# Four attention layers on one core: the first chunk's queries and keys by way of HBM, a reordered beginning, and dense rows for three output projections

## Chip, core and metric

The kernel runs on one core of a Trainium2 chip, alone. The metric is the device time of one execution in microseconds (us); several executions are timed and their median is given. A core has TensorE (matmuls; "PE" in a profile, its weight loads "PEld"), VectorE ("DVE"), ScalarE ("ACT"), GpSimd ("POOL") and SyncE ("SP", which here only issues transfers). Each engine works through its own list of instructions in order, and waits for others by semaphores. SBUF is the on-chip memory, PSUM the memory that matmuls write (eight banks here), HBM the memory outside.

## What is computed

Four layers, each with its own layernorm and a residual: windowed attention (A), full attention (B), A again, B again, over 2048 positions and 640 features, with 32 heads of 20 features. A and B each have one set of weights, used twice.

```
H = 32; Dh = D // H; W = 256                                # D = 640, S = 2048
q, k, v = (x @ wqkv) split by heads
scores = einsum("bhqd,bhkd->bhqk", q, k) * (Dh ** -0.5)
...
mask = (idx[:, None] - idx[None, :] >= 0) & (idx[:, None] - idx[None, :] < W)   # A only
p = softmax(scores)
o = einsum("bhqk,bhkd->bhqd", p, v)
return o.transpose().reshape(B, S, D) @ wo
...
x = A_x
x = x + A(layernorm(x)); x = x + B(layernorm(x))
x = x + A(layernorm(x)); x = x + B(layernorm(x))
```

## The kernel before

**Tiling.** Positions are cut into four chunks of 512 (C), heads into eight groups of four (G). A *unit* (class Unit) is one layer, one chunk of queries and one group: its scores are computed key by query, so that keys lie on the partitions, ACT takes the exponential straight out of PSUM (L1462), and a second matmul with the values (L1495) gives the outputs of four heads, each on 20 of 32 partitions, with the sum of the exponentials on a 21st. The four heads of a group use the four 32-row strips of TensorE at once. For that, the queries and keys of a group lie in a tile of 128 partitions as four strips of 32 rows, 20 with data and 12 with zeros (tiles qa and ka in windowed layers, qt and kt in full ones).

**Order.** One list of units is worked through tile by tile, a tile being three or two banks of scores (an odd tile of layer 0 has two). Layers are interleaved: first the eight units of layer 0, chunk 0, then those of chunk 1; from unit (0, 1, 7) on, the first units of layer 1 alternate with those of chunks 2 and 3, and so on. For each tile the program writes out scores, exponentials, background work, and the values of an earlier tile. Each engine then runs its list in that order; what is written first is done first.

**Background work.** Norms (t_ln), values (t_v), projections to queries and keys (t_block, and t_qk_first for the first chunk) and output projections (t_out) are generators in a queue, todo, sorted by when they are due less a lead (push). pump advances them by an amount per tile: 1.2 units per tile until layer 1's first unit (function rate, before "woven"), and less afterwards. If a unit needs something that isn't written out yet, require writes out tasks until it is there. A yield of ("wait", n) puts a task aside for n tiles. The work after a unit's last values is a tail (t_tail): reciprocals of the sums, spread over the partitions, and a multiplication (L1203), two groups at a time.

**First chunk of layer 0.** first_ln writes out the first norm by hand: statistics on VectorE, the power on POOL, the scaling on ACT, transposes on TensorE, and between them matmuls that nothing reads (warm, L1262). The projections to queries and keys are made group by group by t_qk_first with weights padded to strips of 32 columns (get_w: a POOL memset and a VectorE copy from raw, which lies in the tile spare, to wqk). They land in qa and ka from PSUM by one ACT copy (evac, L345), with no transfer. There are eight groups, so sixteen projections of 5 x 4 matmuls with 512 columns.

**All other chunks.** t_block projects 128 of the 640 rows at a time with unpadded weights, five blocks each for queries and keys. The result goes from PSUM to a staging tile st, and by a transfer on POOL's queue (L566) to HBM (q_d, k_d). load_unit later issues eight transfers on SP's queue per windowed unit (L802, L803), one per head for queries and keys, which place 20 rows into each strip. load_ahead issues them as soon as a unit's blocks are written out and a buffer is free (four qa, eighteen ka).

**Output projection.** t_out works in eight half rows of a chunk (128 positions by 320 features). With padded rows, the outputs of each of the eight groups lie in a slot of the tile on, and the weights wop have zeros in the rows 20 to 31 of each strip; a half row takes 8 x 4 matmuls. With dense rows (function packed: chunks 1 to 3 of layer 3), settle moves the rows of each head by transfers on SP's queue (L1216) into the first five slots of on, and a half row takes 5 x 4. Settling waits two tiles before it issues and eight more after a chunk's last group. Until then a group's raw rows lie in slots 5 to 7, by turns.

**Loads at the start.** SP's queue issues x of chunk 0, the layer A weights in six pieces, the value weights, x of chunks 1 to 3, and the value weights of B, one after the other. t_zeros later writes zeros by POOL's queue into wop and the tiles kt and qt, and loads wop.

## Time and profile before

| | us |
|---|---|
| median of 3 runs | 2161.4 (2161.15 to 2162.79) |
| the profiled execution | 2161.74 |
| its span, first to last instruction | 2160.0 |
| first score matmuls of layer 0 | 16.29 |
| first output projection, first and last addition to x (L598) | 100.06 and 112.33 |
| first score matmul of layer 1 | 148.23 |
| second, third and fourth output projection, first addition | 196.74, 292.43, 386.60 |

The page of the profile gives busy time and share of the span of each engine. In a row by stage there are the stretch, its length, then the busy time of PE, PEld, DVE, ACT and POOL with the number of instructions in brackets, then the granted clock of TensorE (1.00 is full), the share of the transfer engines that is busy, and GB/s. In a row of the timeline there are the start, the time taken by the group of like instructions, engine, line, what is written from what, the count, and in square brackets the idle time before it and what ended that. A row on transfers ends with the KB of one and the median time from issue to landing, where the trace has it; for SP's transfers it has none.

The exponentials alone, by stage (same columns, ACT only):

```profile
16.30:33.70 17.40, 8.98 (x12) 1.00 0.22 75
33.70:86.00 52.30, 32.04 (x45) 1.00 0.48 150
86.00:98.00 12.00, 9.35 (x9) 0.86 0.16 41
98.00:113.00 15.00, 9.33 (x8) 1.00 0.06 16
113.00:155.00 42.00, 30.95 (x25) 1.00 0.19 55
155.00:196.00 41.00, 38.80 (x35) 1.00 0.32 93
```

### The profile page before, as it was taken

The page shows a single profiled execution, that of the slowest core. Times are in us where ns is not written, and L with a number is a line of the kernel's source. Part 1 is how long each engine was busy: PE and PEld are TensorE (multiplying, and loading weights), DVE is VectorE, ACT ScalarE, POOL GpSimd, SP SyncE. Part 2 cuts the span into 40 slices and gives each one's busy share as a digit, 9 for nine tenths or more (in the row PEclk, how much of TensorE's full clock was granted, in tenths as well). Part 3 has the DMA queues.
Part 4 walks back from the last instruction along what each step waited for, and adds up shares of the span by engine and source line. Part 5 has one row for each costly group of instructions (what it writes and reads, how often), then busy time and mean ns, then how long its engine had stood idle before and what let it go on. Part 6 is the DMA issues. An engine that isn't in the chain of part 4 may idle for free. (4 is left out here: it accounts for less than half of the span.)

```text
span 2160.0 us, 73146 instructions
## 1 busy us (share of the span) xinstructions
PE 1926.8 (89%) x31790; PEld 757.8 (35%) x31791; DVE 1467.3 (68%) x2613; ACT 2088.0 (97%) x1717; POOL 361.5 (17%) x805
## 2 busy tenths in 40 slices
PE   8899999988889898888988989888898988888898
PEld 4444443433333333333333433342332222222222
DVE  6556665426666776776767743773588888987886
ACT  7889899999999999999999999999999999999997
POOL 6543434000022002400033001500000000000000
PEclk9999999999999999999999999999999999999999
DMA  6212122222110222111120122111111111111100
GB/s 204 65 54 75 54 62 69 67 63 59 55 42 27 63 53 69 38 31 48 50 83 27 33 60 75 33 45 52 54 57 44 36 36 42 32 33 39 44 27 17
DMA packets 81440, 114.33 MB, mean 53 GB/s; under 512 B 20990, under 2 KB 63070, under 8 KB 81118
## 3 DMA queue, kind: packets, MB, share of 16 engines
q1 hardware_dynamic: 71502, 81.06, 14.2%
q0 software_dynamic: 9616, 28.59, 3.8%
q8 instruction: 249, 4.08, 0.8%
q14 instruction: 73, 0.60, 0.1%
HBM read 76.58 MB, written 27.79 MB: 48 GB/s over the span
## 5 line engine op out<-in xcount | busy, mean ns | idle before, releaser
L1462 ACT ACTIVATE pt<-ps 128x1536 bf16<-128x1536 f32 (+2 forms) x1641 | 2054.0, 1417 | 38.5 <-PE ps L1436 28.9
L1436 PE MATMUL ps<-qt,kt 32*128 32x512 bf16 x3913 | 543.6, 384 | 62.8 <-ACT pt L1462 55.7
L315 PE MATMUL ps<-masks,ident 128*32 128x512 bf16 x5684 | 507.6, 384 | 94.7 <-ACT pt L1462 49.1
L1495 PE MATMUL ps<-pt,vt 128*21 128x512 bf16 x3784 | 377.1, 386 | 0.3 <-ACT pt L1462 0.2
L1436 PEld LDWEIGHTS <-kt 32*128 32x128 bf16 x3913 | 155.5, 91 | 460.1 <-issue 440.8
L315 PEld LDWEIGHTS <-ident 128*32 128x32 bf16 x5684 | 182.2, 94 | 283.4 <-issue 256.7
L1535 POOL TENSOR_SCALAR_AFFINE_SELECT pt<-pt 128x256 bf16<-128x256 bf16 (+2 forms) x508 | 219.0, 453 | 198.6 <-ACT pt L1462 185.8
L348 DVE CAST st<-ps 128x512 bf16<-128x512 f32 x134 | 92.6, 691 | 144.8 <-PE ps L315 144.5
L1495 PEld LDWEIGHTS <-vt 128*21 128x21 bf16 x3784 | 93.7, 89 | 254.2 <-issue 250.5
L315 PE MATMUL ps<-wop,on 128*32 128x320 bf16 x3712 | 160.7, 300 | 4.5 <-DVE x_sb L598 2.6
L1007 DVE TENSOR_SCALAR spare<-ps 128x512 int32<-128x512 f32 x200 | 137.2, 686 | 27.8 <-PE ps L989 24.1
L315 PEld LDWEIGHTS <-on 128*32 128x32 bf16 x5760 | 122.8, 95 | 62.3 <-issue 28.4
L1546 DVE TENSOR_TENSOR pt<-pt,masks 128x256 bf16<-128x256 bf16 (+3 forms) x270 | 117.0, 449 | 39.5 <-ACT pt L1462 37.6
L1436 PE MATMUL ps<-qa,ka 32*128 32x384 bf16 (+2 forms) x1408 | 118.5, 275 | 22.9 <-ACT pt L1462 19.6
L1203 DVE TENSOR_TENSOR on<-on,ps 128x512 bf16<-128x512 bf16 x128 | 86.4, 684 | 59.0 <-PE ps L315 56.9
L598 DVE TENSOR_TENSOR x_sb<-x_sb,ps 128x320 bf16<-128x320 bf16 x120 | 58.3, 486 | 100.3 <-PE ps L315 99.5
L315 PE MATMUL ps<-wv,xnT 128*32 128x320 bf16 x2560 | 117.1, 303 | 9.5 <-DVE on L1203 3.0
L315 PE MATMUL ps<-xnT,spare 128*32 128x512 bf16 x1720 | 118.0, 381 | 5.5 <-DVE on L1203 1.8
L315 PE MATMUL ps<-xnT,wqk 128*32 128x512 bf16 x1600 | 107.7, 381 | 4.6 <-DVE rts L1182 1.3
L1007 DVE TENSOR_SCALAR raw_o<-ps 128x512 int32<-128x512 f32 x112 | 76.8, 686 | 47.6 <-PE ps L1436 46.7
L900 DVE CAST on<-ps 128x512 bf16<-128x512 f32 x112 | 76.7, 685 | 35.5 <-PE ps L1495 28.5
L566 POOL DMA_DIRECT2D k_d<-st x75 | 41.6, 555 | 270.9 <-DVE st L348 248.0
(103 smaller groups left out, 1731.6 us busy)
## 6 DMA issues: line engine op xcount, KB each, us to landing
vt<-v_d SPq DMA_DIRECT2D x48, 336.0 KB
kt<-k_d SPq DMA_DIRECT2D x192, 80.0 KB
k_d<-st POOLq DMA_DIRECT2D x75, 128.0 KB, 2.2
q_d<-st POOLq DMA_DIRECT2D x75, 128.0 KB, 2.1
qt<-q_d SPq DMA_DIRECT2D x384, 20.0 KB
v_d<-vs POOLq DMA_DIRECT2D x16, 336.0 KB, 3.0
qa<-q_d SPq DMA_DIRECT2D x224, 20.0 KB
ka<-k_d SPq DMA_DIRECT2D x224, 20.0 KB
```

Of the source, the lines that this page charges most:

```text
L315: nc.tensor.matmul(out_[r], lhsT=lhsT[:, r], rhs=rhs, start=start, stop=stop)
L348: nc.vector.tensor_copy(out=out_, in_=in_)
L566: nc.gpsimd.dma_start(out=dst, in_=staging.pop())
L598: nc.vector.tensor_tensor(out=xv, in0=had, in1=yp, op=ALU.add)
L900: nc.vector.tensor_copy(out=oT, in_=op)
L1007: nc.vector.tensor_scalar(out=xi.bitcast(I32)[:, i * C : (i + 1) * C], in0=z, scalar1=SCALE * LOG2E * FIX, scalar2=127.5 * FIX, op0=ALU.mu ...
L1203: nc.vector.tensor_tensor(out=oT, in0=oT, in1=zb, op=ALU.mult)
L1436: nc.tensor.matmul(sp[:, i, col * P : (col + qn) * P], lhsT=u.k(kc, j), rhs=u.q(j, q0, qn), start=True, stop=True,)
L1462: nc.scalar.activation(out=pt[:, i:k, b0 * P :], in_=sp[:, i:k, b0 * P :], func=ACT.Exp, scale=SCALE,)
L1495: nc.tensor.matmul(op[32 * j : 32 * j + VW, q0 * P : (q0 + qn) * P], lhsT=u.v(kc, j), rhs=pg[:, i, col * P : (col + qn) * P], start=(first ...
L1535: nc.gpsimd.affine_select(out=v, in_=v, compare_op=ALU.is_gt if later else ALU.is_ge, fill=0.0, base=0, pattern=[[0, k - i], [-1 if later ...
L1546: nc.vector.tensor_tensor(out=pt_[:, i:k, cols], in0=pt_[:, i:k, cols], in1=mv_, op=ALU.mult)
```

## The change

Three things are changed.

**Queries and keys of the first chunk.** Groups 0 and 1 stay with t_qk_first. The rows of groups 2 to 7 are projected by t_block in four blocks (FIRST: rows 160 to 288, 288 to 416, 416 to 544, 544 to 640), staged, written to HBM and loaded per unit like those of other chunks; the last block has three column strips of weights. So (0, 0) needs six padded weight tiles fewer each for queries and keys. The values of the chunk are made in two halves, the second due with group 4. The loaded units use the six ka slots 12 to 17, which VectorE zeroes at the start as before, and two qa slots that it now zeroes as well; ka slots 2 to 7, which chunk 1 uses, are zeroed by two transfers in t_zeros.

**Beginning.** Nine matmuls that nothing reads come ahead of the first norm instead of fourteen, then 2, 3, 3 and 4 instead of 0, 3, 2 and 3. The padded weights of group 0 get their zeros at the start, the query's copy comes before the first copy of the transposed rows and the key's copy after the last. x of chunks 2 and 3 and the value weights of B are loaded from t_zeros, some tiles later; so are the constants that the tails use (end_constants).

**Dense rows.** packed holds for chunks 0 to 2 of layer 0 as well. Their raw rows lie in slots given by PLACE, and a group waits for the settling of the group four before it. wop is loaded dense at first; after the third output projection its padding is zeroed from a zero tensor in HBM and the padded weights are loaded for chunk 3.

```
@@ -44,6 +44,7 @@
 KEEP = 30
+FIRST = ((160, 288), (288, 416), (416, 544), (544, 640))
@@ -122,6 +123,7 @@
     q_d = {l: dram.tile([NC, D, C], BF16, name=f"q_d{l}", tag=f"q_d{l}") for l in range(4)}
+    zero_d = dram.tile([32 - DH, G * D], BF16, name="zero_d", tag="zero_d")
@@ -133,13 +135,23 @@
     nc.sync.dma_start(out=wv_sb[0][:], in_=wq_view[0][:, :, 2 * D : 3 * D])
-    for c in range(1, NC):
+    def load_x(c):
         nc.sync.dma_start(out=x_sb[:, 4 * c : 4 * c + 4, :], in_=xin[:, 4 * c : 4 * c + 4, :])
-    nc.sync.dma_start(out=wv_sb[1][:], in_=wq_view[1][:, :, 2 * D : 3 * D])
+    load_x(1)
...
-        return l == 3 and c > 0
+        return (l == 3 and c > 0) or (l == 0 and c < NC - 1)
+    PLACE = (3, 4, 5, 6, 7, 4, 5, 6)
+    def place(l, c, g):
+        if not packed(l, c) or ((l, c) == (3, NC - 1) and g >= G - 2):
+            return g
+        return PLACE[g] if l == 0 else 5 + g % 3
@@ -169,14 +181,17 @@
+    for n in range(2):
+        nc.gpsimd.memset(
+            wqk[:, :, n * P : (n + 1) * P].rearrange("p c (j m) -> p c j m", j=4)[:, :, :, DH:32], 0.0
+        )
     nc.vector.memset(ka_all[:, G:KA, :], 0.0)
-    def other_constants():
-        nc.vector.memset(op, 0.0)
+    nc.vector.memset(qa_all[:, 2:QA, :], 0.0)
+    def end_constants():
...
         )
@@ -222,7 +237,7 @@
             if name[0] in ("k", "q"):
-                lead = 7 if name[1] == 1 and name[-1] == 0 else 2
+                lead = 7 if name[1] == 1 and name[-1] == 0 else 1 if name[1:] == (0, 0, 2) else 2
@@ -310,7 +325,7 @@
-        for j in range(4):
+        for j in range(lhsT.shape[-1] // 32):
@@ -350,15 +365,19 @@
     worder = {(0, n): [] for n in range(2)}
-    padded = [0]
+    padded = [2]
...
-        a = padded[0] % 8 * P
-        padded[0] += 1
+        if i == 0:
+            a = n * P
+        else:
+            a = padded[0] % 8 * P
+            padded[0] += 1
         tv = t.rearrange("p c (j m) -> p c j m", j=4)
-        nc.gpsimd.memset(tv[:, :, :, DH:32], 0.0)
+        if i > 0:
+            nc.gpsimd.memset(tv[:, :, :, DH:32], 0.0)
@@ -377,8 +396,10 @@
-    def block_w(l, n, b):
+    def block_w(l, n, c, b):
+        if (l, c) == (0, 0):
+            return raw[:, :, n * D + FIRST[b][0] : n * D + FIRST[b][1]]
@@ -400,7 +421,8 @@
                 yield ("hold", 0.22)
-        evac(dst(), pq)
+        m = wt.shape[-1]
+        evac(dst()[0:m], pq[0:m])
@@ -422,7 +444,7 @@
         yield from room("xnT", "ln")
-        users[l, c] = 9 if (l, c) == (0, 0) else (11, 12, 11, 11)[l]
+        users[l, c] = (11, 12, 11, 11)[l]
@@ -484,7 +506,7 @@
         for i in range(4):
-            if windowed:
+            if windowed and 0 in halves:
@@ -531,7 +553,7 @@
-    ka_free = deque(kas)
+    ka_free = deque(kas[0:2] + kas[G + 4 : KA] + kas[2 : G + 4])
@@ -548,10 +570,12 @@
         ready.add(("qk", l, c, g))
-        if g == G - 1:
-            nc.sync.dma_start(out=wqk[:], in_=wq_view[1][:, :, 0 : 8 * P])
-            nc.sync.dma_start(out=wqk_rest, in_=wq_view[1][:, :, 8 * P : 2 * D])
-            ready.add("weights")
+    def load_b():
+        nc.sync.dma_start(out=wqk[:], in_=wq_view[1][:, :, 0 : 8 * P])
+        nc.sync.dma_start(out=wqk_rest, in_=wq_view[1][:, :, 8 * P : 2 * D])
+        ready.add("weights")
@@ -559,12 +583,14 @@
             yield ("wait", 1)
-        wt = block_w(l, n, b)
+        wt = block_w(l, n, c, b)
         yield from project(wt, xnT[l, c], staged)
-        rows = slice(b * P, (b + 1) * P)
+        rows = slice(*FIRST[b]) if (l, c) == (0, 0) else slice(b * P, (b + 1) * P)
         dst = k_d[l][rows, c * C : (c + 1) * C] if n else q_d[l][c, rows, :]
-        nc.gpsimd.dma_start(out=dst, in_=staging.pop())
+        nc.gpsimd.dma_start(out=dst, in_=staging.pop()[0 : rows.stop - rows.start])
         used(l, c)
+        if (l, n, c, b) == (0, 0, 0, len(FIRST) - 1):
+            load_b()
@@ -606,6 +632,12 @@
         n = out_n[0] = out_n[0] + 1
+        if n == NC - 1:
+            for j in range(4):
+                nc.sync.dma_start(
+                    out=wop[32 * j + DH : 32 * j + 32, :, :].rearrange("p g f -> p (g f)"), in_=zero_d[:]
+                )
+            load_wop(0, False)
@@ -653,12 +685,17 @@
             return
-        for g in range(G):
+        for g in range(2):
                 worder[l, n].append((n, g))
-            push(("qk", l, c, g), t_qk_first(l, c, g), need[g], 2.2)
+            push(("qk", l, c, g), t_qk_first(l, c, g), 0, 2.2)
             if g == 0:
-                push(("v", l, c), t_v(l, c, (0, 1)), need[0], 5.6)
+                push(("v", l, c, 0), t_v(l, c, (0,)), 0, 2.8)
+        for b, g in enumerate((2, 3, 5, 6)):
+            if b == 2:
+                push(("v", l, c, 1), t_v(l, c, (1,)), 4, 2.8)
+            for n in (1, 0):
+                push(("qk"[n], l, c, b), t_block(l, n, c, b), g, 1.1)
@@ -777,7 +814,7 @@
     full = deque(u for u in units if not u.windowed)
-    small_units = deque(u for u in units if u.windowed and (u.l, u.c) != (0, 0))
+    small_units = deque(u for u in units if u.windowed and ((u.l, u.c) != (0, 0) or u.g >= 2))
@@ -826,7 +863,13 @@
         if (l, c) == (0, 0):
-            return [("qk", l, c, g)]
+            if g < 2:
+                return [("qk", l, c, g)]
+            return [
+                (n, l, c, b)
+                for b, (r0, r1) in enumerate(FIRST) if r0 < 80 * (g + 1) and r1 > 80 * g
+                for n in "qk"
+            ]
@@ -857,7 +900,7 @@
             require(n)
-        if (u.l, u.c) != (0, 0):
+        if (u.l, u.c) != (0, 0) or u.g >= 2:
@@ -890,10 +933,10 @@
         end = (l, c) == (3, NC - 1) and g >= G - 2
-        before = g - 2 if end else g - 3
+        before = (g - 4 if g >= 5 else -1) if l == 0 else g - 2 if end else g - 3
             require(("tail", l, c, before))
-        oT = ons[l, c][:, 5 + g % 3 if packed(l, c) and not end else g, :]
+        oT = ons[l, c][:, place(l, c, g), :]
@@ -1232,14 +1275,23 @@
         z = ka_all[:, G : G + 4, :].rearrange("p a b -> p (a b)")
-        yield ("wait", 4)
-        for n in range(2):
+        yield ("wait", 3)
+        end_constants()
+        for n in (2, 5):
             nc.gpsimd.dma_start(
-                out=wop[:, 4 * n : 4 * n + 3, :].rearrange("p g f -> p (g f)"), in_=z[:, 0 : 3 * D]
+                out=ka_all[:, n : n + 3, :].rearrange("p a b -> p (a b)"), in_=z[:, 0 : 3 * C]
             )
-            nc.gpsimd.dma_start(out=wop[:, 4 * n + 3, :], in_=z[:, 0:D])
-            yield ("wait", 1)
-        load_wop(0, False)
+        yield ("wait", 1)
+        load_x(2)
+        load_wop(0, True)
+        for n in range(0, G * D, 4 * C):
+            m = min(4 * C, G * D - n)
+            nc.gpsimd.dma_start(out=zero_d[:, n : n + m], in_=z[0 : 32 - DH, 0:m])
+        yield ("wait", 1)
+        yield ("wait", 8)
+        load_x(3)
+        nc.sync.dma_start(out=wv_sb[1][:], in_=wq_view[1][:, :, 2 * D : 3 * D])
+        yield ("wait", 3)
@@ -1253,7 +1305,7 @@
-        users[0, 0] = 9
+        users[0, 0] = 12
@@ -1263,7 +1315,7 @@
-        warm(14)
+        warm(9)
@@ -1298,15 +1350,15 @@
                 trs.append(scale(i - 1))
-                warm((0, 3, 2)[i - 1])
+                warm((2, 3, 3)[i - 1])
+        wtiles[0, 0] = get_w(0, 0)
         trs.append(scale(3))
-        warm(3)
+        warm(4)
         nc.vector.tensor_copy(out=xt[:, :, P : 2 * P], in_=trs[1])
-        for n in (1, 0):
-            wtiles[n, 0] = get_w(n, 0)
         nc.scalar.copy(out=xt[:, :, 3 * P : 4 * P], in_=trs[3])
+        wtiles[1, 0] = get_w(1, 0)
@@ -1316,7 +1368,7 @@
         require(("qk", 0, 0, 0))
-        other_constants()
+        nc.vector.memset(op, 0.0)
@@ -1487,8 +1539,7 @@
                 if first and u.windowed:
-                    require(("v", u.l, u.c, 0))
-                    require(("v", u.l, u.c, 1))
+                    require(("v", u.l, u.c, u.g // 4))
```

## The prediction

> **Views, and what bounds the kernel.** I read the page first, then the busy time by stage (all engines, then the exponentials of L1462 alone), then the timeline of the stages that the change touches.
>
> ```profile
> PE 1926.8 (89%) x31790; PEld 757.8 (35%) x31791; DVE 1467.3 (68%) x2613; ACT 2088.0 (97%) x1717; POOL 361.5 (17%) x805
> ...
> L1462 ACT ACTIVATE pt<-ps 128x1536 bf16<-128x1536 f32 (+2 forms) x1641 | 2054.0, 1417 | 38.5 <-PE ps L1436 28.9
> ```
>
> ACT works 2088.0 of 2160.0 us, 2054.0 of them on exponentials that the change leaves alone. What can be won is the rest of the span, some 106 us. The stages show where it lies (after the colon: length, then busy PE, PEld, DVE, ACT, POOL):
>
> ```profile
> 16.30:33.70 17.40, 16.48 (x329) 8.54 (x330) 5.99 (x15) 13.97 (x25) 7.65 (x20) 1.00 0.22 75
> 33.70:86.00 52.30, 47.99 (x1061) 23.16 (x1058) 30.35 (x87) 44.96 (x76) 30.85 (x75) 1.00 0.48 150
> 86.00:98.00 12.00, 8.57 (x202) 3.97 (x202) 9.38 (x27) 10.73 (x11) 8.46 (x20) 0.86 0.16 41
> 98.00:113.00 15.00, 14.19 (x390) 8.91 (x386) 11.90 (x32) 9.33 (x8) 6.38 (x15) 1.00 0.06 16
> 113.00:155.00 42.00, 38.27 (x961) 19.62 (x953) 23.83 (x52) 38.92 (x47) 21.40 (x52) 1.00 0.19 55
> ...
> 196.00:214.00 18.00, 17.33 (x390) 8.91 (x380) 10.80 (x28) 17.68 (x16) 4.23 (x10) 1.00 0.16 40
> 214.00:262.00 48.00, 44.62 (x966) 20.56 (x963) 31.84 (x69) 40.82 (x35) 17.47 (x43) 0.96 0.15 43
> ...
> 290.00:312.00 22.00, 21.16 (x473) 10.80 (x473) 15.50 (x37) 21.87 (x20) 7.41 (x19) 1.00 0.19 46
> ```
>
> From 16 to 155 us TensorE is fuller than ACT in most rows: projections and the first output projection (98 to 113) pace the exponentials, and ACT is idle there for 20.8 us (the sum of length minus ACT over the first five rows). At 196 to 214 and at 290 to 312, where the second and third output projections run, ACT is full. So work taken off TensorE pays before 155 us and hardly after.
>
> **The change, term by term.** The rows for the costs:
>
> ```profile
> 3.65 5.92 PE L1262 MATMUL ps<-ka,ident 128*128 128x512 bf16 x14 [3.65 <-DVE ka L172]
> ...
> 16.62 0.86 PE L315 MATMUL ps<-wv,xnT 128*32 128x320 bf16 x20
> ...
> 24.00 2.34 PE L315 MATMUL ps<-xnT,wqk 128*32 128x512 bf16 x40
> ...
> 98.74 1.27 PE L315 MATMUL ps<-wop,on 128*32 128x320 bf16 x32 [0.54 <-DVE on L1203]
> ...
> q_d<-st POOLq DMA_DIRECT2D x8, 128.0 KB, 2.1
> ...
> qt<-ka POOLq DMA_DIRECT2D x4, 128.0 KB, 8.0
> ...
> 1860.07 6.69 SPq L1216 DMA_DIRECT2D on<-on  x9
> ```
>
> *Beginning: -1.1 us.* The 14 warming matmuls take 0.42 us each and hold TensorE until 9.4, though the first normalised rows leave ACT near 7.5. Nine end near 7.5. The third row block, which waited for a buffer until 9.94, then waits for its own statistics (the L1272 step at 8.54), and the fourth runs near 10.0 to 10.9 instead of 10.8 to 11.7. The weight copy of the first group moves into VectorE's idle 1.23 us before L1302; the other goes behind the copies, where only the key projection needs it. The first projection then starts near 12.15, not 13.26. Bounds 0 (weights land later than thought) and -1.6 (all the warming time). Two more small memsets on POOL end near 5.5, when the first L1294 starts; the one on VectorE lies in its 0.65 us idle before x arrives.
>
> *Projections: -4.0.* A 20-matmul projection takes 1.17. Out go 12 of them (14.0 us); in come six blocks of 20 and two of 15 (7.0 + 1.8). TensorE is relieved of 5.3 us, ACT of four evictions of 0.58. A part is lost, as a tile of exponentials without work beside it still takes 1.33 us (9 tiles in 86 to 98). With a projection beside it TensorE needs 1.26 + 0.39 + 0.39 = 2.04. The planner spends 1.2 units a tile and 4.4 units go, so 3.7 tiles shrink by 0.71: -2.6. Between -2.6 and -5.3, I take the middle.
>
> *Round trip of groups 2 to 7: +2.0.* TensorE must do the second group (2.34), half the values (4 x 0.86), block 0 (2.34), scores for seven tiles and values for three (10 x 0.39) before block 0's query is out: 15.2 + 12.0 = 27.2. Add eviction 0.58, POOL issue 0.56, landing 2.1: 30.4. SP issues the eight loads 0.37 apart; landing of such a load has no row, and I give it the write's 2.1: the first strip is there at 33.2, the three that the first tile reads at 34.7. Group 2 is due at tile 10, near 32.7, since block 1 (2.34), the rest of 3.6 units of background (0.86) and six matmul groups (2.3) come first. The gap is 2.0 us. Queued behind the waiting scores is all of TensorE, and ACT behind that. With a landing of 0 it is nothing; with the 8.0 of the qt row it is 7.9. Group 3 is due five tiles (10 us) later, its loads five us later, so it has room.
> [...]
>
> *First output projection: -2.8.* Half a row falls from 32 matmuls (1.27) to 20 (0.86, the value row's form), eight times: 3.3 us of TensorE in a stretch where ACT idles 5.7 of 15. Bounds 0 and -3.3.
>
> *Its new wait: +1.5.* The settled rows go through SP: 9 transfers per pair of groups, 6.69 us, and the projection is held back two tiles and eight more, 10 x 1.88 (15 us over 8 tiles) = 18.8 us. It then takes 4.7 tiles instead of 7.5, so its end comes 13.5 us later. TensorE fills the hole with chunk 2's norm, values and blocks, which come after it today. What hangs on it is the first unit of layer 1: the load goes out at 144.41, lands by 146.5, and its score starts at 148.23, so 1.7 us of room. By tiles: ready at 19.5 of chunk 1's 38.4, projected by 24.5, normed by 30, keys and half values by 34.5, written and loaded by 39: about a tile late. Bounds 0 and 13.5 - 1.7 = 11.8. SP's settling (4 x 6.7 us) and loads (24 us for eight units) fit in chunk 1's 69 us.
>
> *Second and third: -0.8 and 0.* 3.3 us of TensorE each, under a full ACT. A little of the second may ease 214 to 262, where ACT loses 7.2 us. Bounds -3.3 and 0 for the second.
>
> *Moved DMAs and constants: 0.* Fewer zeros go out on POOL's queue, and eight block writes at 0.56 replace ten memsets of 0.36. The loads of x 2 and 3 and of layer 1's value weights leave a queue that is full until 20 us (DMA share 1.01) and come back where it idles (0.03); chunk 2's statistics read x only at 83. VectorE drops ten copies. The constants of the tails (2.0 us of small VectorE steps at 14 to 16, POOL memsets of 0.95 and 0.42) move to about tile 9; the first tail reads them near 42, and a mask step behind one waits 0.48 at most. A slot of the packed rows is used again four groups later, some 27 us, and is settled two tiles behind L1203, which follows a group's L900 by 8 us (40.26 to 48.16); no group waits for its slot. Without those 15 us of room the wait would fall on the in-order TensorE in full. If the padded output weights, which come after the third projection, are late, the fourth waits; it starts at 385, over 70 us later.
>
> Sum: -1.1 - 4.0 + 2.0 - 2.8 + 1.5 - 0.8 = -5.2. The profiled execution took 2161.74 us (span 2160.0), so 2156.5; it lies 0.34 above the median of 2161.4, so I forecast 2156.2 for the runs.
>
> **Rivals.**
> (a) Both waits hidden, the terms near their good bounds: -1.6 - 5.3 - 3.3 - 1.6 gives 2149.6. For it: 20.8 us of idle ACT before 155. Against: little lies between block 0 and group 2.
> (b) The tiles keep their pace: only -1.1 and -2.6, with 3.5 us of waits: 2161.2. For it: ACT's 44.96 of 52.3 with 2.3 to lose.
> (c) Slower: layer 1's first unit is late, by the whole 11.8 instead of 1.5. Place: the tail of chunk 0, SP's settling, the ten tiles. After 150 us ACT bounds, so its idle time is not recovered. -6.7 + 11.8 gives 2166.5; it decides from a delay of 6.7 on. For it: the 1.7 us of room. Against: today chunk 2's norm is cut in two by the projection and holds the next one up until 117; it would be done before.
> (d) Slower: the round trip takes the 8.0 landing: 7.9 at group 2, 2.4 at group 3, and 4.7 at group 6, whose loads stand behind 1.6 MB of layer 1's weights (at 340 GB/s). -7.2 + 15.0 gives 2169.2. Against: the 8.0 was under full DMA, and here the engines idle until 30 us.
> The granted clock fell to 0.64 at 218 to 222 after TensorE was busy for 2.21 of 4 us; in (d) some 4 us at that clock add 1.4. [...]
>
> **Chances and range.** Forecast case 0.46 (2153 to 2160, its own range); (a) 0.19; (b) 0.10; (c) 0.17; (d) 0.08. A change below 0.2%, 4.3 us, can't be told from none. Faster by more: (a) and 0.36 of the forecast case, 0.55. Within: 0.20. Slower: (c) and (d), 0.25. The range, 2146 to 2169, takes in (a) to (c).
>
> **What would show it.** Beginning: first scores near 15.2. Projections: 90 fewer 512-wide matmuls and ACT casts to st in place of qa and ka before 60 us. Round trip: TensorE waits about 2 us on a DMA of qa or ka at group 2. Output projection: groups of 20 at 0.86, starting some ten tiles behind L1203. Its wait: the first qt,kt score at 143 to 146. The forecast is wrong if that score comes after 150, if group 2 waits over 6 us, or if ACT idles as long as today before 155.

## Result, and the profile after

The changed kernel takes 2183.3 us (median of 4 runs, 2179.65 to 2186.04) beside 2161.3 of the kernel before (4 runs, 2160.51 to 2162.79): a ratio of 1.0102, 95% interval 1.009 to 1.0114. It is 22 us slower; 2156.2 had been forecast, with a range that ended at 2169. Its profiled execution took 2186.04 us (span 2183.6).

The page of the changed kernel, ACT's exponentials now at L1514:

```profile
PE 1929.4 (88%) x31483; PEld 750.4 (34%) x31484; DVE 1460.0 (67%) x2601; ACT 2087.0 (96%) x1714; POOL 363.4 (17%) x802
...
L1514 ACT ACTIVATE pt<-ps 128x1536 bf16<-128x1536 f32 (+2 forms) x1641 | 2053.2, 1415 | 60.9 <-PE ps L1488 43.4
```

The exponentials take the same 2053 us; ACT's idle time ahead of them grew from 38.5 to 60.9 us, and most of that is waiting for scores. The exponentials alone, by the stages of the table before (length, ACT busy, granted clock, DMA share, GB/s):

```profile
16.30:33.70 17.40, 9.84 (x14) 0.95 0.12 39
33.70:86.00 52.30, 25.88 (x35) 0.86 0.60 193
...
113.00:155.00 42.00, 29.74 (x24) 1.00 0.14 38
155.00:196.00 41.00, 26.83 (x23) 0.88 0.29 86
```

Against the rows before, 33.7 to 86 has 6.2 us of exponentials less and 155 to 196 has 12.0 less, and in both the clock is below full. All engines in the later stages (length, then PE, PEld, DVE, ACT, POOL, clock, DMA share, GB/s):

```profile
214.00:262.00 48.00, 45.43 (x991) 20.88 (x989) 33.15 (x79) 44.83 (x39) 16.95 (x39) 1.00 0.21 57
290.00:312.00 22.00, 19.84 (x335) 8.01 (x332) 12.93 (x27) 19.20 (x17) 10.19 (x23) 0.92 0.31 90
312.00:340.00 28.00, 23.25 (x495) 10.98 (x493) 18.10 (x44) 21.30 (x19) 5.93 (x15) 0.94 0.39 72
```

The kernel before, in the last of these stretches:

```profile
312.00:340.00 28.00, 27.04 (x575) 12.24 (x571) 18.74 (x42) 26.90 (x24) 12.47 (x27) 1.00 0.23 63
```

ACT gains 4.0 us at 214 to 262, where it had 40.82, and loses 2.7 at 290 to 312 (21.87 before) and 5.6 at 312 to 340 (26.90 before). A kernel is called ahead at a time when it has done more microseconds of exponentials by then than the kernel before, and behind when it has done fewer. By the busy time of L1514 summed from the start, the changed kernel is 3.1 us ahead at 30 us, 0.2 behind at 40, 0.7 at 70, 6.4 at 100, 20.4 at 190, 15.8 at 300, 23.9 at 400, and the distance then stays to the end. The losses lie in four places ahead of 340 us. The timeline of the changed kernel shows three of them:

```profile
15.29 0.39 PE L1488 MATMUL ps<-qa,ka 32*128 32x384 bf16 x6 [0.69 <-ACT ka L360]
...
30.87 0.30 SPq L840 DMA_DIRECT2D ka<-k_d  x1
...
32.42 0.60 PE L1488 MATMUL ps<-qa,ka 32*128 32x384 bf16 x2 [2.19 <-DMA ka<-k_d]
...
70.73 8.10 SPq L1259 DMA_DIRECT2D on<-on  x9
...
80.09 0.69 DVE L943 CAST on<-ps 128x512 bf16<-128x512 f32 x1 [9.52 <-DMA on<-on]
80.84 0.80 PE L1546 MATMUL ps<-pt,va 128*21 128x384 bf16 x8 [6.51 <-DVE on L943]
...
82.28 1.45 ACT L1514 ACTIVATE pt<-ps 128x1536 bf16<-128x1536 f32 x1 [7.14 <-issue]
...
165.90 0.58 PE L1488 MATMUL ps<-qt,kt 32*128 32x512 bf16 x1 [6.40 <-DMA kt<-k_d]
```

At 32 TensorE waits for the first loaded strips. At 75 to 82 every engine stands: the eviction to the raw slot (L943) waits for the settling of the pair four groups before, which was multiplied at 49.84 but issued at 70.73, because SP's queue had loads ahead of it and waited itself; TensorE waits for the bank that this eviction frees. The two longest waits of SP's queue from 50 to 71 us are put down to the landing of layer B's query and key weights, issued at 53.46 and 53.91 (who waits for what, then the total in us, how often, the longest):

```profile
SPq L839 <- DMA wqk<-in_B_wqkv_dram: 4.3, 1, 4.3
SPq L840 <- DMA spare<-in_B_wqkv_dram: 2.3, 1, 2.3
```

At 166 the first unit of layer 1 comes 17.7 us later than before. The last multiplication of the first chunk is already 10 us late there (107.95 against 98.00). The fourth place is the third output projection, which waits for its settled rows (1.59 us at 307), and a stop of 2.95 us at 329, for which the profile names no cause.

### The profile page after: what moved, and what is told of

Its sections match the earlier page's. It is cut to its first block, busy times and chain, and to the rows that moved or that the text cites. A ratio compares the mean times of both kernels' runs of the same rounds, so it can differ in the third digit from the quotient of the medians.

```text
span 2183.6 us, 72783 instructions
## 1 busy us (share of the span) xinstructions
PE 1929.4 (88%) x31483; PEld 750.4 (34%) x31484; DVE 1460.0 (67%) x2601; ACT 2087.0 (96%) x1714; POOL 363.4 (17%) x802
## 3 DMA queue, kind: packets, MB, share of 16 engines
q8 instruction: 246, 4.03, 0.8%
## 5 line engine op out<-in xcount | busy, mean ns | idle before, releaser
L1514 ACT ACTIVATE pt<-ps 128x1536 bf16<-128x1536 f32 (+2 forms) x1641 | 2053.2, 1415 | 60.9 <-PE ps L1488 43.4
L330 PE MATMUL ps<-masks,ident 128*32 128x512 bf16 x5756 | 515.2, 385 | 94.2 <-ACT pt L1514 49.2
L330 PE MATMUL ps<-wop,on 128*32 128x320 bf16 x3424 | 152.2, 302 | 6.6 <-DVE x_sb L624 3.9
L1488 PE MATMUL ps<-qa,ka 32*128 32x384 bf16 (+2 forms) x1408 | 121.7, 280 | 20.7 <-ACT pt L1514 16.4
L330 PEld LDWEIGHTS <-on 128*32 128x32 bf16 x5472 | 115.3, 95 | 63.4 <-issue 29.5
L330 PE MATMUL ps<-xnT,spare 128*32 128x512 bf16 x1870 | 130.2, 385 | 6.8 <-DVE on L1246 2.4
L943 DVE CAST on<-ps 128x512 bf16<-128x512 f32 x112 | 76.8, 685 | 49.0 <-PE ps L1546 30.9
L330 PE MATMUL ps<-xnT,wqk 128*32 128x512 bf16 x1360 | 94.1, 386 | 4.2 <-DVE rts L1225 1.3
```

What stands on the lines that cost most here:

```text
L330: nc.tensor.matmul(out_[r], lhsT=lhsT[:, r], rhs=rhs, start=start, stop=stop)
L943: nc.vector.tensor_copy(out=oT, in_=op)
L1488: nc.tensor.matmul(sp[:, i, col * P : (col + qn) * P], lhsT=u.k(kc, j), rhs=u.q(j, q0, qn), start=True, stop=True,)
L1514: nc.scalar.activation(out=pt[:, i:k, b0 * P :], in_=sp[:, i:k, b0 * P :], func=ACT.Exp, scale=SCALE,)
```

## The experiments

All times come from comparisons that hold the kernel before too. Its median is 2160.8 to 2162.3 in them, so a difference between runs of two comparisons is uncertain by about 1 us. "Addition" is the first L598 of the first chunk, "score" the first qt,kt matmul, both in us.

| run | median | ratio, 95% interval | addition | score |
|---|---|---|---|---|
| before | 2161.3 | | 100.06 | 148.23 |
| changed | 2183.28 | 1.0102, 1.009 to 1.0114 | 128.03 | 165.90 |
| e1_padded | 2167.3 | 1.003, 1.002 to 1.0039 | 104.85 | 153.02 |
| e2_dense_only | 2172.44 | 1.0054, 1.0038 to 1.0071 | 118.68 | 157.09 |
| e3_bulk_pool | 2180.61 | 1.0082, 1.0061 to 1.0104 | 123.78 | 161.74 |
| e4_no_hold | 2181.37 | 1.0086, 1.007 to 1.0102 | 121.49 | 163.61 |
| e5_padded_early | 2163.77 | 1.0014, 1.0004 to 1.0023 | 102.32 | 150.50 |
| e6_padded_early_fill | 2162.7 | 1.0005, 0.9995 to 1.0014 | 103.14 | 152.92 |
| e7_beginning | 2166.48 | 1.002, 1.0009 to 1.0031 | 98.56 | 152.34 |
| e8_early_loads | 2176.65 | 1.0077, 1.0062 to 1.0092 | 123.47 | 161.60 |
| e9_spread_reload | 2174.5 | 1.0064, 1.0049 to 1.0079 | 121.36 | 159.27 |
| e10_split_settle | 2163.65 | 1.0019, 1.0009 to 1.0028 | 114.92 | 153.07 |
| e14_split_hold8 | 2168.7 | 1.0036, 1.0022 to 1.005 | 119.53 | 157.46 |
| e11_padded_first_chunk | 2162.08 | 1.0007, 0.9998 to 1.0016 | 101.07 | 149.25 |
| e13_padded_first_split | 2162.56 | 1.0008, 0.9999 to 1.0017 | 99.19 | 149.10 |
| e12_all_mended | 2160.26 | 0.9997, 0.9988 to 1.0006 | 112.81 | 150.13 |
| e15_short_wait | 2158.66 | 0.9988, 0.9979 to 0.9997 | 105.64 | 145.71 |

**Parts alone.** The first theory was that the dense rows cost the time, its rival that the round trip and the half clock set off everything.

```
e1  -  return (l == 3 and c > 0) or (l == 0 and c < NC - 1)
    +  return l == 3 and c > 0          (wop zeroed and loaded padded in t_zeros)
e2     the kernel before with packed, place, settling and reload of the change, no blocks
```

> The changed kernel, but layer 0's output projections stay padded (no settling, no dense weights, no reload after the third). Theory A (the dense rows cost the time: groups that wait for their slot, a late first unit of layer 1, late loads after the third projection): 2157 to 2161 us, no stop at 75 to 82, first layer-1 score before 150. Rival B (the round trip through HBM at group 2 and the half clock after it set off everything): 2170 or more.

> The kernel before with the dense rows of layer 0 alone (slots, settling, dense weights first, padded reload after the third projection). Theory A: 2170 to 2187 us, with a wait for a slot or a late first unit of layer 1. Rival B: 2156 to 2163.

Without dense rows 16 of the 22 us are gone, but 6 are left, between the two expectations: neither theory covers the whole. Dense rows alone cost 11 us, as expected. The two parts together make 17.5 of the 22; the wait for the slot at 75 to 82 is in neither, as it takes both the settling and the late loads on SP's queue. The place of the loss in e2_dense_only is narrow: exponentials run level with before within 1.5 us until 144, and are 11.6 behind at 180. Its timeline (the two steps of line 451 and 443 belong to the norms of chunk 2 and of layer 1):

```profile
98.61 1.28 DVE L1218 TENSOR_TENSOR on<-on,ps 128x512 bf16<-128x512 bf16 x2 [1.85 <-PE ps L324]
99.32 6.86 SPq L1231 DMA_DIRECT2D on<-on  x9
...
99.81 0.45 DVE L451 TENSOR_SCALAR xn<-x_sb,rstd,nmr 128x640 bf16<-128x640 bf16 x1
...
118.68 0.49 DVE L607 TENSOR_TENSOR x_sb<-x_sb,ps 128x320 bf16<-128x320 bf16 x1 [0.89 <-PE ps L324]
...
133.67 0.24 DVE L443 SCALAR_TENSOR_TENSOR nmr<-mv,rstd 128x4 f32<-128x4 f32 x1
...
157.09 0.58 PE L1449 MATMUL ps<-qt,kt 32*128 32x512 bf16 x1 [6.93 <-DMA kt<-k_d]
```

The same steps in the kernel before:

```profile
98.00 1.28 DVE L1203 TENSOR_TENSOR on<-on,ps 128x512 bf16<-128x512 bf16 x2 [1.73 <-PE ps L315]
...
100.06 0.49 DVE L598 TENSOR_TENSOR x_sb<-x_sb,ps 128x320 bf16<-128x320 bf16 x1 [0.78 <-PE ps L315]
...
114.58 0.65 DVE L442 TENSOR_SCALAR xn<-x_sb,rstd,nmr 128x640 bf16<-128x640 bf16 x1
...
122.55 1.08 DVE L434 SCALAR_TENSOR_TENSOR nmr<-mv,rstd 128x4 f32<-128x4 f32 x1
...
148.23 0.39 PE L1436 MATMUL ps<-qt,kt 32*128 32x512 bf16 x1
```

The last multiplication of the first chunk is about where it was (98.61 against 98.00), and the addition to x comes 20.1 us behind it instead of 2.1: 0.7, then 6.9 us of settling on SP, its landing, and the rest of the ten tiles. 38.4 us after the addition comes the score, and TensorE has nothing else to do for the last 6.93.

**Where e1_padded loses 6 us.** Its busy times in 2 us steps (columns as above), and the timeline at the stop:

```profile
70.00:72.00 2.00, 2.00 (x53) 1.18 (x49) 0.69 (x2) 2.00 (x6) 1.08 (x4) 1.00 1.12 175
72.00:74.00 2.00, 0.97 (x18) 0.23 (x11) 0.77 (x4) 1.88 (x5) 1.10 (x4) 1.00 1.11 167
74.00:76.00 2.00, 0.00 (x0) 0.00 (x0) 0.00 (x0) 0.00 (x0) 0.24 (x1) 1.00 0.96 318
76.00:78.00 2.00, 1.31 (x20) 0.82 (x20) 0.00 (x0) 0.05 (x1) 0.00 (x0) 0.60 0.66 244
```

```profile
76.69 1.22 PE L329 MATMUL ps<-wv,xnT 128*32 128x320 bf16 x13 [3.72 <-issue]
```

TensorE stops in the middle of a projection, 7 matmuls done and 13 to go, waiting for nothing that the profile shows, while the transfer engines are full; one packet of the instruction queue moves in that time. The loads that the change put there were taken back to the start, with and without dense rows:

```
    load_x(1)                 ->   for c in range(1, NC): load_x(c)
                                   nc.sync.dma_start(out=wv_sb[1][:], ...)
    (load_x(2), load_x(3) and wv_sb[1] taken out of t_zeros)
```

> As e1_padded (first layer from padded rows, beginning and blocks as in the changed kernel), but x 2, x 3 and the value weights of half B are loaded in the first microseconds, as in the kernel before. In e1_padded every engine stood still at 74 to 76 us with the DMA share at 1.05 to 1.12 from 68 to 74. Theory A (the bulk loads put later fill the DMA engines and TensorE's own next instructions come late): the stop at 73 to 77 and the half clock behind it go, exps stay level with before until 90 instead of 4.6 us behind, time 2161 to 2164. Rival B (the stop belongs to the blocks and their zero writes, not to the bulk loads): it stays, 2166 to 2168.

> The changed kernel whole, dense rows too, but x 2, x 3 and the value weights of half B loaded in the first microseconds as before. Theory A (the late bulk loads hold SP's queue, the settling waits for its issue until 70.7 and the stop at 75 to 82 follows): the settling is issued by 62, the stop goes, exps are 3 us further at 90, time 2176 to 2180 with the cliff at 160 still there. Rival B (the settling is late by the unit loads and the B weights alone): 2181 to 2184.

The times are those of Theory A in both: 3.5 us are won with padded rows, 6.6 with dense ones. With padded rows the half clock behind the stop is gone (1.00 from 76 to 78 instead of 0.60), but exponentials are 2.8 us behind at 90 instead of level, and the stop is only shorter. In e5_padded_early TensorE is busy for 1.92 us from 72 to 74 and for 0.49 from 74 to 76, where e1_padded has 0.97 and 0.00.

With dense rows the settling is issued at 63.14, not by 62, and the eviction that stood in the changed kernel no longer waits for it; but the next one, at 84.10, waits 4.20 us for the next pair, and exponentials fall 3.3 us back from 80 to 90. SP's queue is still not free enough. What TensorE stands for at 74 to 76 is not shown: that its next instructions come late, as Theory A of e5_padded_early has it, was the author's guess. The transfer engines need not be full for such a stop: from 74 to 76 us their share is 0.13 in e5_padded_early (0.96 in e1_padded).

The same loads moved to POOL's queue, and the wait behind the last settling cut from 8 tiles to 1:

```
e3   nc.sync.dma_start(...)   ->  nc.gpsimd.dma_start(...)     x 3, wv_sb[1], weights of B
e4   yield ("wait", 8)        ->  yield ("wait", 1 if l == 0 else 8)
```

> The changed kernel, but layer B's query/key and value weights and x of chunk 3 are issued on POOL's queue instead of SP's. If SP's queue, held by these bulk loads, makes the settling of groups 0 and 1 late: the stop at 75 to 82 goes, 2174 to 2178 us. If the settling itself is too slow or is written out too late: within 2 us of the changed kernel, 2181 to 2185.

> The changed kernel, but a chunk of layer 0 is held back one tile instead of eight after its last settling transfers are written out. If the hold delays the chain to layer 1: first layer-1 score 5 to 10 us earlier, 2174 to 2178 us. If the hold only covers what the transfers take anyway: TensorE waits for them at the first projection instead, 2180 to 2186.

Each moved the time by 2 to 3 us, inside the intervals. In e3_bulk_pool the settling is issued at 63.41 instead of 70.73, but the eviction at 83.86 waits 4.42 us for the next pair, and the time that its first theory gave did not come. In e4_no_hold the score is 2.3 us earlier, not 5 to 10, and the wait went onto TensorE, as its second theory said:

```profile
112.98 6.42 SPq L1259 DMA_DIRECT2D on<-on  x8
...
115.64 0.73 PE L330 MATMUL ps<-wop,on 128*32 128x320 bf16 x16
...
120.91 0.46 PE L330 MATMUL ps<-wop,on 128*32 128x320 bf16 x4 [4.55 <-issue]
```

Sixteen of the twenty matmuls of a half row run; the last four come 4.55 us later. The profile names nothing that they wait for, but they read the rows whose transfers SP is still giving out until 119.4. So a shorter wait alone wins nothing that can be measured as long as the settling is that slow.

**The settling.** Half of its transfers then went over POOL's queue, first with the wait cut to 5 tiles, then with that left at 8:

```
e10, e14   nc.sync.dma_start(out=on[...], ...)  ->  (nc.gpsimd if l == 0 and j % 2 else nc.sync).dma_start(...)
e10        yield ("wait", 8)                    ->  yield ("wait", 5 if l == 0 else 8)
```

> As e8_early_loads, but the settling's transfers go half over SP's queue and half over POOL's, and the wait behind the last settling is 5 tiles instead of 8. In e2_dense_only the first addition to x came 18.6 us later than before (118.68 against 100.06) and the first score of layer 1 at 157.09 instead of 148.23. Theory A (settling and wait make the first layer's output late, and with it layer 1's first unit): that score, at 161.6 in e8_early_loads, comes at 153 to 157, time 2169 to 2173. Rival B (the first unit is late by other work put ahead of it): it stays near 161, time 2175 to 2178.

> As e10_split_settle, but the wait behind the last settling is 8 tiles again, as in the changed kernel: only the two queues are left of that edit. e8_early_loads took 2176.65, e10_split_settle 2163.65, its first layer-1 score at 153.07 against 161.60. Theory A (SP's queue, held 7 us by each settling, is most of it; the shorter wait is worth at most its 3 tiles, 4 us): 2163 to 2168, that score at 153 to 157. Rival B (the wait of 8 tiles is most of it, the queues little): 2171 to 2176, score at 158 or later.

```profile
100.08 3.21 SPq L1262 DMA_DIRECT2D on<-on  x4
101.03 2.63 POOL L1262 DMA_DIRECT2D on<-on  x5
...
114.92 0.49 DVE L626 TENSOR_TENSOR x_sb<-x_sb,ps 128x320 bf16<-128x320 bf16 x1 [1.77 <-PE ps L332]
...
153.07 0.48 PE L1488 MATMUL ps<-qt,kt 32*128 32x512 bf16 x1 [3.82 <-DMA kt<-k_d]
```

The lines are of e10_split_settle. A pair is given out in 3.6 us instead of 7. The two edits give 13.0 us, which is 5 us more than Theory A of e10_split_settle expected. Of these, 8.0 are for the queues (2176.65 to 2168.7, 0.7 above Theory A's range in e14_split_hold8, with the score of 157.46 half a microsecond behind it), and 5.0 for the three tiles, where at most 4 were expected. The queues are clear of the noise; the intervals of e14_split_hold8 and e10_split_settle overlap, so the size of the second part is not sharp, though the score moves by 4.4 us. The queues bring more than the 4 us of the earlier score. That fits that settlings also stand in front of unit loads: in e2_dense_only one holds SP from 158.25 to 165.4, in the middle of layer 1's first loads.

**The reload of wop.**

```
e9   for j in range(4):  yield ("wait", 4); zeros of strip j;  yield ("wait", 4); weights of strip j
```

> As e8_early_loads, but the eight transfers that put the padded output weights back after the third output projection are given out one at a time, four tiles apart, instead of all at once. Theory A (those eight, on SP's queue and on the DMA engines together, make the layer-1 loads and TensorE's instructions late and cost about 5 us between 300 and 340): exps stay level there, time 2171 to 2174. Rival B (the loss at 300 to 340 is the wait for the settling, or shifted work, not the reload): 2175 to 2178.

Theory A was wrong on the place. The time fell by 2.2 us, to between the two ranges and within the intervals, but from 300 to 320 exponentials fall back by 4.7 us as in e8_early_loads (4.6), where TensorE waits 2.04 us for settled rows. In e10_split_settle, with the reload in one piece, they lose 1.0 there. So the loss at the third projection was the wait for its settled rows, not the reload.

**The gap at group 2.** Eight matmul groups that nobody reads were put ahead of its first scores:

```
e6   if (u.l, u.c, u.g) == (0, 0, 2): state["owed"] += 8
```

> As e5_padded_early, with 8 more matmul groups that nobody reads ahead of group 2's first scores, where TensorE stands 2.19 us for the DMA in the changed kernel and its granted clock is 0.50 right after. Theory A (the gap drops the clock, and that costs about 3.3 us more than the gap): the clock stays at 1.00 from 32 to 40, exps are about 3 us further at 40, and the time is 2 to 4 us under e5_padded_early. Rival B (ScalarE is behind for the 2 us wait alone, the clock costs nothing): within 1 us of e5_padded_early.

Busy times of the changed kernel, and then of e6_padded_early_fill:

```profile
30.00:34.00 4.00, 1.81 (x26) 0.78 (x25) 3.83 (x9) 1.47 (x3) 3.61 (x8) 0.74 0.34 106
34.00:38.00 4.00, 4.00 (x56) 1.59 (x52) 2.99 (x9) 2.50 (x4) 3.32 (x7) 0.50 0.82 259
```

```profile
30.00:34.00 4.00, 3.45 (x65) 1.52 (x53) 3.81 (x9) 1.88 (x4) 3.62 (x7) 1.00 0.38 106
34.00:38.00 4.00, 3.66 (x78) 1.89 (x78) 2.81 (x8) 2.89 (x5) 3.86 (x9) 1.00 0.94 347
```

The clock stays at 1.00 instead of 0.50, and exponentials are 1.1 us further than before at 40 instead of level with it. The time gained only 1.1 us, between the two theories and inside the intervals. In the profiled execution the lead is down to 0.1 us at 60; TensorE then stands for 2.29 of the 5 us from 70 to 75, and exponentials are 2.4 behind at 80. The clock's fall is shown, the 3 us that it was thought to cost are not.

**The beginning alone.**

> The kernel before with the reordered beginning alone (order of the first weights, zeros of the first padded weights early, 9 warming matmuls, the first chunk's values in two halves); no blocks, no dense rows, loads where they were. Theory A (the head is worth its 1.0 us, and the values in halves give 3 us of exps more by 30 that last): 2157 to 2160.5. Rival B (what is won at the head is lost again at the projections of 35 to 80): 2161 to 2163.

Both theories missed. The lead of 3.1 us at 30 lasts until 90 (3.3), longer than any version with blocks keeps it, and is then lost: 2.4 behind at 148, 7.9 at 200. TensorE waits 1.05 us for a copy of ACT at 144, the next half row of keys takes 2.17 instead of 1.26 us with the clock at 0.50, and the clock is at 0.50 again at 170 to 172 and 197 to 199. Why these stops come here and not in the kernel before stayed open.

**Dense rows where nobody waits.** With the first projection padded, the second and third dense:

```
e11  return (l == 3 and c > 0) or (l == 0 and 0 < c < NC - 1)   (on e6, wop swapped after n == 1 and, as in e9, n == 3)
e13  e11 with the settling of e10
```

> As e6_padded_early_fill, but the first layer's second and third output projections from dense rows (the first stays padded); the dense weights are loaded after the first projection, the padded ones put back one transfer at a time after the third. Theory A (dense rows cost only where layer 1's first unit waits for them; at the second projection, 210 to 260, they give back about 3 us): 2158.5 to 2161, under the kernel before. Rival B (the settling holds SP's queue 7 us at a time wherever it is, and that costs as much as the lighter projections give): 2163 to 2167.

> As e11_padded_first_chunk (first projection padded, second and third from dense rows, bulk loads at the start, 8 idle matmul groups), with the settling over both queues. Theory A (no layer-1 unit waits, and the settling holds no queue for 7 us): 1 to 3 us under e11_padded_first_chunk, 2158 to 2161, and under the kernel before. Rival B (with the first chunk padded, SP's queue had room; what is left of e11_padded_first_chunk is its stop at 70 to 90): 2161 to 2163.

The first (2162.08) lies between the two expectations, the second (2162.56) in its rival's: no layer-1 unit waits, and the lighter projections still give nothing that can be measured over e6_padded_early_fill (2162.7).

**All mended, and a shorter wait.**

```
e12  e8 + two queues and 5 tiles (e10) + spread reload (e9) + 8 groups at group 2 (e6)
e15  yield ("wait", 5 if l == 0 else 8)  ->  yield ("wait", 2 if l == 0 else 8)
```

> The changed kernel with everything that the other runs point to put right, dense rows kept for all three chunks: bulk loads at the start, 8 idle matmul groups ahead of group 2, the settling over two queues with a wait of 5 tiles, the padded weights put back one at a time. Theory A (these are separate losses that add up): about 2163 to 2168. Rival B (one late start is behind them all, and they do not add up): 2171 or more.

> As e12_all_mended, but the wait behind the last settling is 2 tiles instead of 5. In e12_all_mended TensorE stands 2.99 us for kt before layer 1's first score at 150.13, its clock falls, and exps go from 1.6 us ahead of before at 140 to 4.5 behind at 160. Theory A (that wait still sets layer 1's first unit): the score comes 3 us earlier, no wait for kt, exps stay level or ahead at 160, time 2156 to 2159, under the kernel before. Rival B (the wait only moves to TensorE, in front of the projections, as in e4_no_hold): 2160 to 2164.

e12_all_mended came out under what Theory A gave: level with before. It still lost 6 us of exponentials at 140 to 160, with a wait of 2.99 us for kt. The last run takes that away:

```profile
96.85 3.21 SPq L1265 DMA_DIRECT2D on<-on  x4
97.80 2.63 POOL L1265 DMA_DIRECT2D on<-on  x5
...
105.64 0.49 DVE L626 TENSOR_TENSOR x_sb<-x_sb,ps 128x320 bf16<-128x320 bf16 x1 [1.41 <-PE ps L332]
...
145.71 0.39 PE L1493 MATMUL ps<-qt,kt 32*128 32x512 bf16 x1
```

There is no wait for kt, the score comes at 145.71, and exponentials are 1.6 us ahead of before at 160 and 3.9 at 400, as Theory A said. It runs in 2158.66 beside 2162.26 of before in the same comparison: 0.12% faster, interval 0.03 to 0.21%, less than the 0.2% called a difference here, but faster than both kernels. The interval overlaps that of e12_all_mended, so the 1.6 us between these two runs are not shown; that the score moved and the wait went is.

## Why the prediction was wrong

**Right.** The first scores come at 15.29 (forecast 15.2). There are 90 matmuls of 512 columns fewer (3230 against 3320 on xnT). Dense half rows take 0.86. The addition comes 20.1 us behind the multiplication (18.8). The wait at group 2 was 2.19 us (2.0), but that match is partly luck: it began at 30.23 instead of 32.7, its load landed at most some 1.3 us after issue (30.87 plus the 0.30 of its issue, to 32.42) instead of 2.1, and TensorE went on before the third strip's load was given out (32.34 to 32.67).

**The step that failed most: "Its new wait: +1.5", with bounds 0 and 11.8.** The wait itself was sized well, what hangs on it was not. In e2_dense_only the addition is 18.6 us later and the score 8.9; TensorE stands 6.93 us for it, the clock is 0.50 from 156 to 160 (0.62 and 0.60 in the 4 us before and after), and exponentials fall back by about 12.

The step that failed is the chain from the settled rows to layer 1's first score. The forecast counted it in tiles, 19.5 of them from "ready at 19.5" to "loaded by 39", and took the end to be "about a tile late". At its own 1.88 us a tile this chain is 36.7 us; from the end of the wait (98.00 + 18.8 = 116.8) it ends at 153.5, some 5 us behind the 148.23 of before, not 1.5. Measured, the score follows the addition by 38.4 us in e2_dense_only, and by 37 to 42 us in every run whose first projection is dense, however early or late the addition is; in the kernel before it follows by 48.2. So there were about 10 us of room, and a wait of 18 can't hide in it.

Rival (c) had this mechanism. Its reason against was right in fact, but too small: chunk 2's norm is indeed done before (its last row at 99.81 instead of 114.58), and layer 1's norm then follows the first addition by 15.0 us instead of 22.5, which is most of the 10 us of room. Its price, 11.8, was somewhat low: the two edits of e14_split_hold8 and e10_split_settle alone take 13.0 us off this term.

**"No group waits for its slot. Without those 15 us of room the wait would fall on the in-order TensorE in full."** The wait fell on TensorE, at 75 to 82. The 15 us were counted from when the settling could be issued, two tiles behind the multiplication at 49.84, so near 53.6 at 1.88 us a tile; SP's queue gave it out only at 70.73, some 17 us later. Rival (d) counted layer 1's 1.6 MB of weights in front of group 6's loads; the term on the slot counted no queue.

**"Moved DMAs and constants: 0."** The loads were meant for a stretch that was idle before (0.03). They came out elsewhere: x of chunk 2 at 40.40, x of chunk 3 and the value weights of B at 68.88 and 69.33, directly ahead of the settling and behind a stretch with a share of 0.96 and 1.04 (55 to 65). From 70 to 75 the share is 0.90, where it was 0.17 before. Moved back to the start, they are worth 6.6 us (e8_early_loads) with dense rows, in part through the slot, and 3.5 us without.

**The gap at group 2, counted without a loss of clock.** The forecast's +2.0 has no term for the clock. No run with such a gap shows that it costs none: the granted clock fell to 0.50 in the changed kernel's gap of 2.19 us, with TensorE busy for 1.81 of the 4 us from 30 to 34, and it is 0.50 from 34 to 38 behind the gaps of e1_padded (2.39 us) and e5_padded_early (2.32 us) as well. The prediction's own row, 0.64 after 2.21 of 4 us, already pointed there.

**"Projections: -4.0" and "Beginning: -1.1".** With a wait of 2 us these should have left a lead of 3.1 us behind the first chunk's projections. Blocks gained nothing by 70 us: e7_beginning, without blocks, is 2.9 us ahead of before there, e5_padded_early 0.7 behind, and e15_short_wait, with its filled gap, 1.6 ahead. The beginning brings its 1.0 us at the first scores, but alone, in e7_beginning, it ends 4.6 us slower than the kernel before, and why stays open.

**Output projections: the first -2.8, the second -0.8.** In e15_short_wait exponentials gain 0.8 us on before from 100 to 120, less than the first was forecast to give, and 2.4 from 200 to 280. The 2.4 can't be credited to the second: e6_padded_early_fill, with padded rows, gains as much there. The third gave nothing, as forecast.

**The sum of the runs.** From 2183.3 the loads at the start take 6.6, two queues 8.0, three tiles of wait 5.0, the filled gap and the spread reload together 3.4, three more tiles 1.6, which ends at 2158.7. Each step but the fourth compares runs of two comparisons; set against the kernel before in its own, the steps are 7.2, 6.9, 5.2, 3.4 and 2.9. That e15_short_wait gains 3.6 us, where 5.2 were forecast, does not bear the forecast out: it is another kernel, and the terms have other sizes. In these runs the change pays only where the settling is quick (3.6 us a pair) and nothing stands in front of it.

## What to carry to other kernels

A transfer has two prices: the time to land (2.1 us for q_d<-st in the kernel before), and the time that its issue holds the queue (0.76 us for a settling transfer on SP); a 7 us string of small transfers on a queue that also feeds the units has to be weighed as work on that queue. When a wait is put into a chain, measure the chain from that point to its next consumer (here 48 us, 38 of them needed) rather than counting its work in tiles. A mean DMA share says little about a queue (it is 0.60 from 33.7 to 86 in the changed kernel, where SP gave the settling out some 17 us late): look at the stretch where the moved transfer will stand, and at what waits behind it.

## What was not expected of the hardware

In the changed kernel TensorE's clock fell to half at 31.95, 1.7 us into a gap of 2.19 us, and was back at 38.8, 6.8 us later, though TensorE had been busy for most of that time (4.00 of the 4 us from 34 to 38). In e1_padded, with the transfer engines full (share 0.96 to 1.12), TensorE stood for 3.72 us in the middle of a projection with nothing to wait for that the profile shows; with the loads moved, in e5_padded_early, it was still idle for 1.51 of the 2 us from 74 to 76. What it stood for is not shown: the instruction queue moves one packet from 72 to 78 in e1_padded (246 of 16.4 KB, 4.03 MB, in the whole of the changed kernel), and no run isolates whether that one was late. A settling transfer, 20 rows or fewer from SBUF to SBUF, holds SP for about 0.76 us (6.86 over 9) and POOL for 0.53 (2.63 over 5), a unit's load 0.33.
